# Chunked attention, then a low-rank mixer: q and k of later tiles turned by VectorE instead of TensorE

## The chip, the cores and the metric

The kernel runs on one core of a Trainium2 chip. The metric is device time in microseconds (us), from launch to end, and lower is better. Engines are named as the profile names them: PE (TensorE matmuls) and PEld (its weight loads), DVE (VectorE), ACT (ScalarE), POOL (GpSimd), SP (SyncE, which here only issues DMAs).

## The reference

```python
# q, k, v: (8, 8, 576, 64) float32: batch, heads, sequence, head dim; chunks of 64 positions
scores = scale * q_c @ k_c.T            # within each chunk only
attn = exp(scores - max) / (sum + 1e-9)
x = (attn @ v_c), heads joined          # (8, 576, 512)
xt = x.transpose(0, 2, 1)
u = x + (xt @ U @ V).transpose(0, 2, 1) # U (576, 32), V (32, 576)
out = u + relu(u @ w_ch1) @ w_ch2       # w_ch1 (512, 2048), w_ch2 (2048, 512)
```

U, V and the weights arrive as 64-bit floats and are turned into 32-bit ones on the chip. Where precision needs it, a 32-bit operand is split into a high and a low part (names ending in `h` and `l`), and a product becomes three matmuls.

## The kernel before

The batch of 8 is worked on in four pairs of sequences (`pr` = 0 to 3). A pair has 2 x 576 = 1152 positions, which are nine tiles (`t` = 0 to 8) of 128; tile 4 spans the two sequences. A tile (`pr`, `t`) goes through attention: q and k are loaded with the positions in the partitions (`load_qk`, tiles `qn`, `kn`), turned by four PE transposes of 128x128 each into `ps_qT` and `ps_kT` in PSUM (L419), copied to SBUF by ACT as `qT`, `kT` (L433), multiplied into scores (`sc`, L441), run through the softmax on DVE and ACT (`mx`, `ex`), turned again (`ps_eT`, `eT`) and multiplied by v (`av`, L472). The result is `x`. The low-rank part (`y`, `u`) and one more transpose (`ut`) follow.

Nearly all PE work is the mixer behind it. The columns of the hidden layer are cut into 16 blocks (`f`), the tiles of a pair into three groups of three (`g`). One block is `hidden` (twelve matmuls `h` of 128x384, L638), relu with the split into `hh` on ACT and `hl` on DVE, and `project_out` (nine matmuls `o` of 128x512, L664). There are 4 x 3 x 16 = 192 blocks. The attention of later tiles is woven into the blocks of earlier ones.

Two things set the order. Everything of pair 0, with the rounding of the weights from 64 to 32 bits and the first two tiles of pair 1, is placed by a small planner: an `Op` has an engine, a cost, predecessors and the buffers that it takes, and `order()` plays the list through and writes the instructions down in the order of their starts. After that, `plan()` lists the steps of each group of 16 blocks and spreads them over the blocks; there the framework's scheduler settles the order within each engine's queue, with a priority to what was written first.

Three things matter for what follows. Pair 0's nine tiles are "early": they have buffers of their own (`qkv`), and the change leaves them alone. The other 27 tiles take `qn`, `kn`, `vn`, `qT`, `kT`, `ex`, `eT` from eight shared buffers (`slot`). And all of their loads, the weight loads (`wraw`, L325 and L329) and the stores of the result go through SP's queue in order: an instruction there that waits holds up all behind it. Each DMA from SP also counts its completion on one of eight semaphores in turn, and waits until the DMA eight places before it on that queue has landed.

In the chain of a weight block, `wraw` is loaded, ACT begins the rounding (L86), five DVE instructions end it (L101), and ACT and DVE split it into `w` (L348, L351). The blocks that need weight block `f` come in the order of `STRETCHES`: for two groups in turn, so that a weight block serves two blocks of 4.2 us.

Of the kernel before, what the change touches and what calls it, by code (L numbers as in the profile page):

```python
# [10 lines left out]
F32 = mybir.dt.float32  # L11
# [10 lines left out]
def kernel(  # L22
# [11 lines left out]
    nc = tc.nc  # L34
    B, H, S, D = q.shape
# [19 lines left out]
    NPAIR = B // 2  # L55
# [13 lines left out]
    def slot(dtype, name, shape=(P, 512)):  # L69
        return work.tile(list(shape), dtype, tag="slot", name=name, bufs=NS)  # L70
# [40 lines left out]
    rank = [0]  # L111
# [260 lines left out]
    x_of = {}  # L372
    y_of = {}
    ut_of = {}

    def load_qk(pr, t):
        n = f"{pr}_{t}"
        if early(pr, t):
            words = wslot((4 * DM,), F32, "qkv_" + n)
            qn, kn = (words[:, z * DM : (z + 1) * DM].rearrange("p (h d) -> p h d", h=H) for z in range(2))  # L380
            vn = words[:, 2 * DM : 2 * DM + H * D1].rearrange("p (c a k) -> p c a k", c=2, k=D1)
        else:
            qn = slot(F32, "qn_" + n, (P, H, D))
            kn = slot(F32, "kn_" + n, (P, H, D))
            vn = slot(F32, "vn_" + n, (P, 2, HP, D1))
        nc.gpsimd.memset(vn[:, :, :, D:], 1.0)  # L386
        for r, m, b, s0 in segments(pr, t):
            nc.sync.dma_start(qn[r : r + m], q[b, :, s0 : s0 + m, :].rearrange("h s d -> s h d"))
            nc.sync.dma_start(kn[r : r + m], k[b, :, s0 : s0 + m, :].rearrange("h s d -> s h d"))
        loaded[pr, t] = qn, kn, vn  # L390

    def load_v(pr, t, behind=None):
        vn = loaded[pr, t][2]
        for c in range(2):
            b, s0 = divmod(t * P + c * C, S)
            b += 2 * pr
            for e in range(2):
                queue = nc.gpsimd if early(pr, t) else nc.sync
                d = queue.dma_start(
                    vn[e * C : (e + 1) * C, c, :, 0:D],  # L400
                    v[b, e::2, s0 : s0 + C, :].rearrange("h s d -> s h d"),
                )
                if behind is not None and c == e == 0:
                    sync = mybir.DependencyInfo(mybir.DependencyClass.Sync, mybir.DependencyReason.DATA)
                    tc.add_manual_dep(d.ins, behind.ins.name, sync, reason="q and k go first")

    def load(pr, t):
        load_qk(pr, t)
        load_v(pr, t)

    def attention_ops(pr, t, after=None):
        n = f"{pr}_{t}"
        st = {}
        mine = early(pr, t)

        def transpose(src, name):
            ps = st[name] = bank("ps_" + name + n)
            for j in range(4):
                o = nc.tensor.transpose(  # L419
                    ps[:, j * P : (j + 1) * P], src[:, j * P : (j + 1) * P], ident  # L420
                )
            if mine and name == "qT_":
                q_last[t] = o

        def evacuate(name):
            if name[0] == "e" or not mine:
                dst = slot(F32, name + n, (P, HP, P))
            elif name[0] == "q":
                st["qk"] = wslot((2, HP, P), F32, "qkT_" + n)
                dst = st["qk"][:, 0]  # L430
            else:
                dst = st["qk"][:, 1]
            nc.scalar.copy(dst.rearrange("p a b -> p (a b)"), st[name])  # L433
            st[name] = dst
# [51 lines left out]

        def scaled(e):
            if e == 0:
                st["x"] = work.tile([P, HP, 2, D], F32, tag="x", name="x_" + n, bufs=NX)
            nc.vector.tensor_mul(  # L490
                st["x"][:, :, e, :],
                st["av"][e][:, :, 0:D],
                st["sm"][:, e].unsqueeze(2).broadcast_to([P, HP, D]),
            )
            if e == 1:
                x_of[pr, t] = st["x"].rearrange("p a b k -> p (a b k)")

        src = lambda z: loaded[pr, t][z].rearrange("p h d -> p (h d)")
        flat = lambda: st["ex"].rearrange("p a b k -> p (a b k)")
        lq = Op("SP", 3.4, lambda: load_qk(pr, t), after, take="w" if mine else "slot slot slot", lat=1.6)  # L500
        tq = Op("PE", 0.55, lambda: transpose(src(0), "qT_"), lq, begun.get((pr, t - 2)), take="bank")
        lv = Op(
            "POOL" if mine else "SP",
            2.5,
# [2 lines left out]
            lat=2.2,  # L507
        )
        if mine:
            tqs[t], lvs[t] = tq, lv  # L510
        cq = Op("ACT", 0.58, lambda: evacuate("qT_"), tq, take="w" if mine else "slot", free="bank")
        tk = Op("PE", 0.55, lambda: transpose(src(1), "kT_"), lq, tq, take="bank")
        ck = Op("ACT", 0.58, lambda: evacuate("kT_"), tk, cq, take="" if mine else "slot", free="bank")
        sc = Op("PE", 0.62, scores, ck, take="bank bank", free="w" if mine else "slot slot slot slot")
        m0 = Op("DVE", 0.41, lambda: maximum(0), sc, take="slot mx")
        s0 = Op("DVE", 0.41, lambda: subtract(0), m0, free="bank")
        m1 = Op("DVE", 0.41, lambda: maximum(1), s0)
        s1 = Op("DVE", 0.41, lambda: subtract(1), m1, free="bank mx")
        ex = Op("ACT", 0.63, exp, s1)
        te = Op("PE", 0.55, lambda: transpose(flat(), "eT_"), ex, take="bank", free="slot")  # L520
        ce = Op("ACT", 0.58, lambda: evacuate("eT_"), te, take="slot", free="bank")
# [2 lines left out]
        x0 = Op("DVE", 0.415, lambda: scaled(0), sm, free="bank")  # L524
        x1 = Op("DVE", 0.415, lambda: scaled(1), x0, free="bank sm")
        begun[pr, t] = te
        return [[lq, lv], [tq, cq], [tk, ck], [sc, m0, s0, m1, s1, ex], [te, ce], [av, sm, x0, x1]]

    ybank = {}
    q_last, tqs, lvs, ahead = {}, {}, {}, {}  # L530
# [99 lines left out]
    def hidden(pr, g, f):  # L630
        uh, ul = ut_of[pr, g]
        ps = bank(f"h_{pr}_{g}_{f}")
        w = w1[f]
        prods = [(0, uh), (0, ul), (1, uh)]
        n = 0
        for cc in range(NCC):
            for z, u in prods:
                nc.tensor.matmul(  # L638
                    ps[:, :GN], lhsT=w[:, z, cc], rhs=u[:, cc, :], start=(n == 0), stop=(n == 3 * NCC - 1)
                )  # L640
                n += 1
        return ps
# [75 lines left out]
    WORK = "U T3 T4 T8 T5 T2 T1 T7 T0 T6 W0 P0 P1 V M0 M1 W1 W2 W3 W4 W5 W6 W7 W8 W9 W10 W11 W12 W13 W14 W15".split()  # L718
    STRETCHES = ((0, 0, 2), (1, 0, 2), (0, 2, 3), (1, 2, 3), (0, 3, 4), (1, 3, 4), (0, 4, 5), (1, 4, 5), (0, 5, 6), (1, 5, 6), (0, 6, 7), (1, 6, 7), (0, 7, 8), (1, 7, 8), (0, 8, 9), (1, 8, 9), (0, 9, 10), (1, 9, 10), (0, 10, 11), (1, 10, 11), (0, 11, 12), (1, 11, 12), (0, 12, 13), (1, 12, 13), (0, 13, 14), (1, 13, 14), (0, 14, 16), (1, 14, 16))
    GATES = (28, 30)  # L720
    BASE = 1000
    u_done = None
    v_done = []
# [30 lines left out]
        lvs[b].after.append(tqs[a])  # L754
    prev = None
    blocks = 0
    gates = dict(zip(GATES, range(len(GATES))))
    for g, f0, f1 in STRETCHES:
        for f in range(f0, f1):
            rank[0] = BASE  # L760
            prev = block_ops(0, g, f, f == 0, f == NF - 1, [*w_done[f], *mixed[g]], prev)
            blocks += 1
            if (g, f) == (0, NF - 1):
                last = prev
            if blocks in gates:
                rank[0] = 0
                attention_ops(1, gates[blocks], prev[0])
    assert blocks == 2 * NF
    rank[0] = 0
    for t in range(6, NT):  # L770
# [122 lines left out]
```

## Time and profile before

| | |
|---|---|
| runs | 1002.82 us median of three (1000.29 to 1005.15) |
| profiled execution | span 1000.9 us from the first to the last instruction; no time of its own is given outside the span |
| PE busy | 980.2 us (98%) |
| DVE busy | 405.6 us (41%) |
| ACT busy | 256.9 us (26%) |
| mean granted PE clock | 0.994 |
| q and k loads of the 27 later tiles | 60 DMAs, 256 KB each (128 KB where a tile spans two sequences) |

A row of a group of instructions gives the line, engine and operation, output and inputs, shape, count, then busy time and the mean of one in ns, then the idle time of the engine just before and what ended it. A row of the timeline or of the chain gives start, length, and the instruction, with a count where several stand together. A row of a window gives its bounds and length, the busy time of PE, PEld, DVE, ACT and POOL with instruction counts, the granted clock, the mean busy share of the 16 DMA engines, and GB/s.

### The profile page before, as it was taken

How to read it: one execution, taken by the hardware profiler on the slowest of the kernel's cores; microseconds unless marked ns; L12 is line 12 of the kernel's file. 1: busy time of each engine (PE TensorE's matmuls, PEld its weight loads, DVE VectorE, ACT ScalarE, POOL GpSimd, SP SyncE). 2: the span in 40 equal slices, each digit the busy share in tenths (PEclk: the TensorE clock that was granted, in tenths of full speed). 3: DMA queues.
4: the chain of work that ended last, by engine and by line, in shares of the span. 5: the costliest groups of instructions: out<-in, count | busy, mean ns of one | idle time of the engine just before them, and what ended most of it. 6: DMA issues, size and time to landing. Idle time of an engine off the chain costs nothing.

```text
span 1000.9 us, 16704 instructions
## 1 busy us (share of the span) xinstructions
PE 980.2 (98%) x7073; PEld 854.2 (85%) x7073; DVE 405.6 (41%) x813; ACT 256.9 (26%) x460; POOL 33.3 (3%) x89
## 2 busy tenths in 40 slices
PE   7799999999999999999999999999999999999998
PEld 4569999888888889888888898888888889989997
DVE  5789999652332434222333332322423233211211
ACT  4533433322322222221222221221322221111110
POOL 6500000000000000000000000000000000000000
PEclk8999999999999999999999999999999999999999
DMA  9962223152312102121120111021021000000000
GB/s 223 225 207 73 97 84 115 23 148 54 64 33 64 32 5 60 32 46 52 35 62 35 30 32 32 35 62 33 32 65 32 32 1 1 32 1 1 32 1 32
DMA packets 121914, 56.42 MB, mean 56 GB/s; under 512 B 106208, under 2 KB 114432, under 8 KB 121840
## 3 DMA queue, kind: packets, MB, share of 16 engines
q1 hardware_dynamic: 120320, 52.18, 20.5%
q0 software_dynamic: 1520, 3.17, 1.5%
q8 instruction: 56, 0.92, 0.4%
q14 instruction: 18, 0.15, 0.0%
HBM read 45.83 MB, written 9.51 MB: 55 GB/s over the span
## 4 chain that ended last, share of the span: by engine, by line
PE 71%; DVE 0%; ACT 0%; DVEq 0%; issue 0%; ACTq 0%
PE h L638 31%; PE o L664 31%; PE av L472 1%; PE sc L441 1%; PE ut L604 1%; PE ps_eT L419 1%; PE ps_qT L419 1%; PE ps_kT L419 1%; PE u L592 1%; PE y L552 1%; PE y L553 1%; DVE x L676 0%; DVE ex L459 0%; ACT ex L463 0%; DVEq L888 0%; DVE mx L455 0%
## 5 line engine op out<-in xcount | busy, mean ns | idle before, releaser
L638 PE MATMUL h<-uth,w 128*128 128x384 f32 x1536 | 425.2, 341 | 0.4 <-DVE x L490 0.3
L664 PE MATMUL o<-w,hh 128*128 128x512 f32 x1152 | 363.5, 403 | 0.0
L638 PEld LDWEIGHTS h<-uth,w 128*128 128x128 f32 x1536 | 281.3, 188 | 8.5 <-issue 0.8
L651 DVE SCALAR_TENSOR_TENSOR hl<-h,hh 128x384 fp32r<-128x384 f32 x192 | 106.7, 556 | 429.9 <-ACT hh L646 429.8
L638 PE MATMUL h<-utl,w 128*128 128x384 f32 x768 | 259.4, 338 | 0.0
L664 PEld LDWEIGHTS o<-w,hh 128*128 128x128 f32 x1152 | 207.7, 188 | 34.9
L646 ACT ACTIVATE hh<-h 128x384 fp32r<-128x384 f32 x192 | 94.3, 491 | 481.9 <-PE h L638 481.8
L664 PE MATMUL o<-w,hl 128*128 128x512 f32 x576 | 217.7, 395 | 0.0
L638 PEld LDWEIGHTS h<-utl,w 128*128 128x128 f32 x768 | 144.4, 188 | 6.3 <-DVE utl L617 0.3
L664 PEld LDWEIGHTS o<-w,hl 128*128 128x128 f32 x576 | 108.3, 188 | 24.8
L463 ACT ACTIVATE ex<-ex 128x512 f32<-128x512 f32 x36 | 22.7, 632 | 87.4 <-DVE ex L459 87.3
L455 DVE TENSOR_REDUCE mx<-sc 128x4 f32<-128x256 f32 x72 | 27.9, 417 | 31.7 <-PE sc L441 31.7
L598 DVE TENSOR_TENSOR x<-u,x 128x512 f32<-128x512 f32 x36 | 24.3, 684 | 27.1 <-PE u L592 26.8
L617 DVE TENSOR_TENSOR utl<-ut,uth 128x512 fp32r<-128x512 f32 x36 | 24.4, 688 | 20.3 <-ACT uth L612 20.3
L433 ACT COPY eT<-ps_eT 128x512 f32<-128x512 f32 x36 | 21.0, 587 | 37.4 <-PE ps_eT L419 37.2
L545 DVE TENSOR_TENSOR xl<-x,xh 128x512 fp32r<-128x512 f32 x30 | 20.5, 688 | 23.6 <-ACT xh L541 20.5
L612 ACT CAST uth<-ut 128x512 fp32r<-128x512 f32 x36 | 20.8, 588 | 31.6 <-PE ut L604 31.6
L459 DVE TENSOR_TENSOR ex<-sc,mx 128x256 f32<-128x256 f32 x72 | 27.9, 417 | 1.2 <-DVE mx L455 0.5
L490 DVE TENSOR_TENSOR x<-av,sm 128x256 f32<-128x256 f32 x72 | 27.2, 418 | 1.1
L386 POOL MEMSET vn<- 128x8 f32 x27 | 3.0, 113 | 698.9 <-PE y L553 171.1
L676 DVE TENSOR_TENSOR x<-o,x 128x512 f32<-128x512 f32 x36 | 23.3, 684 | 5.8 <-PE o L664 5.8
L348 ACT CAST w<-wroom 128x1024 fp32r<-128x1024 f32 (+1 forms) x19 | 17.1, 915 | 27.4 <-DVE wroom L101 27.4
(88 smaller groups left out, 606.6 us busy)
## 6 DMA issues: line engine op xcount, KB each, us to landing
wraw<-in_moe_w_ch_dram SPq DMA_DIRECT2D x32, 512.0 KB, 4.7
out_dram<-x SPq DMA_DIRECT2D x36, 256.0 KB, 2.1
vn<-in_v_dram SPq DMA_DIRECT2D x108, 64.0 KB, 2.8
qn<-in_q_dram SPq DMA_DIRECT2D x24, 256.0 KB, 3.4
kn<-in_k_dram SPq DMA_DIRECT2D x24, 256.0 KB, 4.0
qkv<-in_v_dram POOLq DMA_DIRECT2D x36, 64.0 KB, 6.6
qkv<-in_q_dram SPq DMA_DIRECT2D x8, 256.0 KB, 8.9
qkv<-in_k_dram SPq DMA_DIRECT2D x8, 256.0 KB, 8.0
```

Of the source, the lines that this page charges most:

```text
L419: o = nc.tensor.transpose(ps[:, j * P : (j + 1) * P], src[:, j * P : (j + 1) * P], ident)
L455: nc.vector.reduce_max(mx, st["sc"][e], axis=AX.X)
L459: nc.vector.tensor_sub(st["ex"][:, :, e, :], st["sc"][e], mx.unsqueeze(2).broadcast_to([P, HP, C]))
L463: nc.scalar.activation(exf, exf, AF.Exp, scale=SCALE)
L490: nc.vector.tensor_mul(st["x"][:, :, e, :], st["av"][e][:, :, 0:D], st["sm"][:, e].unsqueeze(2).broadcast_to([P, HP, D]),)
L598: nc.vector.tensor_add(x, st["u"], x)
L617: nc.vector.tensor_sub(ul[:, :, js], st["t"].rearrange("p (c t) -> p c t", c=NCC), uh[:, :, js])
L638: nc.tensor.matmul(ps[:, :GN], lhsT=w[:, z, cc], rhs=u[:, cc, :], start=(n == 0), stop=(n == 3 * NCC - 1))
L646: nc.scalar.activation(hh, ps[:, :GN], AF.Relu)
L651: nc.vector.scalar_tensor_tensor(hl, ps[:, :GN], 0.0, hh, op0=ALU.max, op1=ALU.subtract)
L664: nc.tensor.matmul(acc[g, j], lhsT=h[:, js], rhs=w2[f][:, z], start=(first and i == 0), stop=(final and i == 2),)
L676: nc.vector.tensor_add(x, ps, x)
```

## The change

For the 27 later tiles, q and k no longer go through PE. DVE can transpose, but only within squares of 32x32. So the data is brought into an arrangement in which that is enough: a new function `halve` copies half of the head dim (32 of 64 values) of q or k of one sequence from HBM to an HBM scratch tensor `half...` of shape (576, 8 x 32), in runs of 128 B; there are eight such transfers for a pair, 24 in all. `load_qk` then reads from the scratch 32 positions at a time into 32 partitions, in runs of 512 B, with four DMAs for each of q and k (eight for the tile that spans two sequences). Two DVE instructions (`squares`, L460) turn `qn` and `kn` into `qT` and `kT`. The heads now stand in another order (0 to 3 in the upper partitions, 4 to 7 in the lower, instead of even and odd ones), and v's loads and x's columns follow (`heads`).

Each `halve` waits for the last `hidden` matmul written before it. For pair 1 the planner places the eight transfers, one after each block from the fourth on; for pairs 2 and 3 they are written behind the load of the next tile, one or two per tile. The planner's first tiles of pair 1 wait for the last of the eight.

```diff
+    def halve(b, z, g):
+        d = halves[b, z, g] = dram.tile([S, H * SQ], F32, name=f"half{'qk'[z]}_{b}_{g}")
+        moved = nc.sync.dma_start(
+            d.rearrange("s (h i) -> s h i", h=H),
+            (q, k)[z][b, :, :, g * SQ : (g + 1) * SQ].rearrange("h s i -> s h i"),
+        )
+        sync = mybir.DependencyInfo(mybir.DependencyClass.Sync, mybir.DependencyReason.DATA)
+        tc.add_manual_dep(moved.ins, hidden_last[0].ins.name, sync, reason="after this block")
+
+    def halvings(pr):
+        return [lambda b=b, z=z, g=g: halve(b, z, g) for b in (2 * pr, 2 * pr + 1) for z in range(2) for g in range(2)]
...
+        if not early(pr, t):
+            for z, dst in enumerate((qn, kn)):
+                for r, m, b, s0 in segments(pr, t):
+                    for e in range(2):
+                        for g in range(2):
+                            x0 = (2 * e + g) * SQ
+                            nc.sync.dma_start(
+                                dst[x0 : x0 + SQ, r // SQ : (r + m) // SQ, :],
+                                halves[b, z, g][s0 : s0 + m, e * P : (e + 1) * P].rearrange(
+                                    "(a j) c -> j a c", j=SQ
+                                ),
+                            )
...
+        def squares(z, name):
+            dst = slot(F32, name + n, (P, HP, P))
+            nc.vector.transpose(
+                dst.rearrange("p h (a j) -> p h a j", j=SQ),
+                loaded[pr, t][z].rearrange("p a (h i) -> p h a i", i=SQ),
+            )
+            st[name] = dst
...
+        if mine:
+            cq = Op("ACT", 0.58, lambda: evacuate("qT_"), tq, take="w", free="bank")
...
+        else:
+            ck = Op("DVE", 0.6, lambda: squares(1, "kT_"), tq, take="slot")
+            turned = [[tq], [ck]]
...
+    HALVES_FROM = 4
...
+            if blocks >= HALVES_FROM and second:
+                rank[0] = 0
+                in_halves = Op("SP", 0.6, second.pop(0), prev[0], lat=6.0)
...
+                pr, t = tiles[i]
+                if pr + 1 < NPAIR:
+                    todo = to_halve.setdefault(pr + 1, halvings(pr + 1))
+                    for _ in range(-(-len(todo) // max(1, NT - 1 - t))):
+                        todo.pop(0)()
```

PE, in a regular stretch of pair 1's mixer, at tile 1 of pair 2. Before, between the hidden blocks 4 and 5 of group 1:

```order
L638 MATMUL h_1_4_4038<-uth_1_3622,w_1207 128x384
L419 MATMUL ps_qT_1_4055<-ident,qn_1_3695 128x128 x4
L664 MATMUL o_3_3947<-w_1141,hh_1_3_4008 128x512 x2
L664 MATMUL o_3_3947<-w_1141,hl_1_3_4010 128x512
L664 MATMUL o_4_3951<-w_1141,hh_1_3_4008 128x512 x2
L664 MATMUL o_4_3951<-w_1141,hl_1_3_4010 128x512
L664 MATMUL o_5_3955<-w_1141,hh_1_3_4008 128x512 x2
L664 MATMUL o_5_3955<-w_1141,hl_1_3_4010 128x512
L419 MATMUL ps_kT_1_4071<-ident,kn_1_3696 128x128 x4
L638 MATMUL h_1_5_4078<-uth_1_3622,w_1273 128x384
```

Now:

```order
L690 MATMUL h_1_4_4052<-uth_1_3630,w_1213 128x384
L716 MATMUL o_3_3953<-w_1143,hh_1_3_4014 128x512 x2
L716 MATMUL o_3_3953<-w_1143,hl_1_3_4016 128x512
L716 MATMUL o_4_3957<-w_1143,hh_1_3_4014 128x512 x2
L716 MATMUL o_4_3957<-w_1143,hl_1_3_4016 128x512
L716 MATMUL o_5_3961<-w_1143,hh_1_3_4014 128x512 x2
L716 MATMUL o_5_3961<-w_1143,hl_1_3_4016 128x512
L690 MATMUL h_1_5_4082<-uth_1_3630,w_1283 128x384
```

The two groups of four transposes are gone, and the `o` matmuls after the fourth hidden block still read the `hl` of the third.

SP among the weight loads (`wraw_1093` and the next ones are weight blocks 7, 8 and so on). Before:

```order
L325 DMA wraw_1093<-in_moe_w_ch_dram 128x4x256
L329 DMA wraw_1093<-in_moe_w_ch_dram 128x1024
L325 DMA wraw_1162<-in_moe_w_ch_dram 128x4x256
L329 DMA wraw_1162<-in_moe_w_ch_dram 128x1024
L325 DMA wraw_1228<-in_moe_w_ch_dram 128x4x256
L329 DMA wraw_1228<-in_moe_w_ch_dram 128x1024
```

Now:

```order
L326 DMA wraw_1093<-in_moe_w_ch_dram 128x4x256
L330 DMA wraw_1093<-in_moe_w_ch_dram 128x1024
L382 DMA halfq_0_1120<-in_q_dram 4608x1x32
L382 DMA halfq_1_1162<-in_q_dram 4608x1x32
L326 DMA wraw_1166<-in_moe_w_ch_dram 128x4x256
L330 DMA wraw_1166<-in_moe_w_ch_dram 128x1024
L382 DMA halfk_0_1190<-in_k_dram 4608x1x32
L382 DMA halfk_1_1232<-in_k_dram 4608x1x32
L326 DMA wraw_1236<-in_moe_w_ch_dram 128x4x256
L330 DMA wraw_1236<-in_moe_w_ch_dram 128x1024
```

Ahead of each of the weight blocks 8, 9, 10 and 11 stand two transfers that were not there.

SP at tile 4 of pair 1, the one that spans two sequences. Before:

```order
L679 DMA out_dram<-x_5_737 128x512
L399 DMA vn_4_2354<-in_v_dram 64x4x64
L388 DMA qn_4_2352<-in_q_dram 64x8x64
L389 DMA kn_4_2353<-in_k_dram 64x8x64
L388 DMA qn_4_2352<-in_q_dram 64x8x64
L389 DMA kn_4_2353<-in_k_dram 64x8x64
L399 DMA vn_4_2354<-in_v_dram 64x4x64 x3
```

Now, from the last loads of tile 3 to the seventh and eighth of q:

```order
L432 DMA vn_3_2298<-in_v_dram 64x4x64 x4
L382 DMA halfq_0_2312<-in_q_dram 4608x1x32
L382 DMA halfq_1_2314<-in_q_dram 4608x1x32
L409 DMA qn_4_2366<-halfq_0_1120 32x2x128
L409 DMA qn_4_2366<-halfq_1_1162 32x2x128
L409 DMA qn_4_2366<-halfq_0_1120 32x2x128
L409 DMA qn_4_2366<-halfq_1_1162 32x2x128
L409 DMA qn_4_2366<-halfq_0_1257 32x2x128
L409 DMA qn_4_2366<-halfq_1_1302 32x2x128
L409 DMA qn_4_2366<-halfq_0_1257 32x2x128
L409 DMA qn_4_2366<-halfq_1_1302 32x2x128
```

Two transfers for pair 2 stand ahead of the tile's loads; the seventh and eighth load of q are eight places behind them, and eight loads of k and four of v follow.

More of the change, by code (lines that the diff above doesn't have):

```diff
@@ L41 @@
     C = 64
+    SQ = 32
     D1 = D + 1
@@ L374 @@
     ut_of = {}
+    halves = {}
+    hidden_last = [None]
+    def halve(b, z, g):
[8 more added lines that the diff above has]
+        return [lambda b=b, z=z, g=g: halve(b, z, g) for b in (2 * pr, 2 * pr + 1) for z in range(2) for g in range(2)]
     def load_qk(pr, t):
@@ L382, in load_qk @@
         else:
-            qn = slot(F32, "qn_" + n, (P, H, D))
-            kn = slot(F32, "kn_" + n, (P, H, D))
+            qn = slot(F32, "qn_" + n, (P, P // SQ, P))
+            kn = slot(F32, "kn_" + n, (P, P // SQ, P))
             vn = slot(F32, "vn_" + n, (P, 2, HP, D1))
         nc.gpsimd.memset(vn[:, :, :, D:], 1.0)
+        if not early(pr, t):
[10 more added lines that the diff above has]
+                            )
+            loaded[pr, t] = qn, kn, vn
+            return
         for r, m, b, s0 in segments(pr, t):
@@ L390, in load_qk, with heads @@
         loaded[pr, t] = qn, kn, vn
+    def heads(pr, t, e):
+        return slice(e, None, 2) if early(pr, t) else slice(e * HP, (e + 1) * HP)
     def load_v(pr, t, behind=None):
@@ L400, in load_v @@
                     vn[e * C : (e + 1) * C, c, :, 0:D],
-                    v[b, e::2, s0 : s0 + C, :].rearrange("h s d -> s h d"),
+                    v[b, heads(pr, t, e), s0 : s0 + C, :].rearrange("h s d -> s h d"),
                 )
@@ L409, in load, with attention_ops @@
         load_v(pr, t)
-    def attention_ops(pr, t, after=None):
+    def attention_ops(pr, t, *after):
         n = f"{pr}_{t}"
@@ L423, in transpose @@
                 q_last[t] = o
+        def squares(z, name):
[5 more added lines that the diff above has]
+            st[name] = dst
         def evacuate(name):
-            if name[0] == "e" or not mine:
+            if name[0] == "e":
                 dst = slot(F32, name + n, (P, HP, P))
@@ L488, in scaled @@
             if e == 0:
-                st["x"] = work.tile([P, HP, 2, D], F32, tag="x", name="x_" + n, bufs=NX)
+                st["x"] = work.tile([P, DM], F32, tag="x", name="x_" + n, bufs=NX)
+            by_head = st["x"].rearrange("p (h d) -> p h d", h=H)
             nc.vector.tensor_mul(
-                st["x"][:, :, e, :],
+                by_head[:, heads(pr, t, e), :],
                 st["av"][e][:, :, 0:D],
@@ L495, in scaled @@
             if e == 1:
-                x_of[pr, t] = st["x"].rearrange("p a b k -> p (a b k)")
-        src = lambda z: loaded[pr, t][z].rearrange("p h d -> p (h d)")
+                x_of[pr, t] = st["x"]
+        src = lambda z: loaded[pr, t][z].rearrange("p a b -> p (a b)")
         flat = lambda: st["ex"].rearrange("p a b k -> p (a b k)")
-        lq = Op("SP", 3.4, lambda: load_qk(pr, t), after, take="w" if mine else "slot slot slot", lat=1.6)
-        tq = Op("PE", 0.55, lambda: transpose(src(0), "qT_"), lq, begun.get((pr, t - 2)), take="bank")
+        lq = Op(
+            "SP", 3.4 if mine else 5.0, lambda: load_qk(pr, t), *after, take="w" if mine else "slot slot slot", lat=1.6
+        )
+        if mine:
+            tq = Op("PE", 0.55, lambda: transpose(src(0), "qT_"), lq, begun.get((pr, t - 2)), take="bank")
+        else:
+            tq = Op("DVE", 0.6, lambda: squares(0, "qT_"), lq, begun.get((pr, t - 2)), take="slot")
         lv = Op(
@@ L510, in attention_ops @@
             tqs[t], lvs[t] = tq, lv
-        cq = Op("ACT", 0.58, lambda: evacuate("qT_"), tq, take="w" if mine else "slot", free="bank")
-        tk = Op("PE", 0.55, lambda: transpose(src(1), "kT_"), lq, tq, take="bank")
-        ck = Op("ACT", 0.58, lambda: evacuate("kT_"), tk, cq, take="" if mine else "slot", free="bank")
+        if mine:
+            cq = Op("ACT", 0.58, lambda: evacuate("qT_"), tq, take="w", free="bank")
+            tk = Op("PE", 0.55, lambda: transpose(src(1), "kT_"), lq, tq, take="bank")
+            ck = Op("ACT", 0.58, lambda: evacuate("kT_"), tk, cq, free="bank")
+            turned = [[tq, cq], [tk, ck]]
+        else:
+            ck = Op("DVE", 0.6, lambda: squares(1, "kT_"), tq, take="slot")
+            turned = [[tq], [ck]]
         sc = Op("PE", 0.62, scores, ck, take="bank bank", free="w" if mine else "slot slot slot slot")
@@ L526, in attention_ops @@
         begun[pr, t] = te
-        return [[lq, lv], [tq, cq], [tk, ck], [sc, m0, s0, m1, s1, ex], [te, ce], [av, sm, x0, x1]]
+        return [[lq, lv], *turned, [sc, m0, s0, m1, s1, ex], [te, ce], [av, sm, x0, x1]]
     ybank = {}
@@ L637, in hidden @@
             for z, u in prods:
-                nc.tensor.matmul(
+                hidden_last[0] = nc.tensor.matmul(
                     ps[:, :GN], lhsT=w[:, z, cc], rhs=u[:, cc, :], start=(n == 0), stop=(n == 3 * NCC - 1)
@@ L756 @@
     blocks = 0
+    second = halvings(1)
     gates = dict(zip(GATES, range(len(GATES))))
@@ L764 @@
                 last = prev
+            if blocks >= HALVES_FROM and second:
+                rank[0] = 0
+                in_halves = Op("SP", 0.6, second.pop(0), prev[0], lat=6.0)
             if blocks in gates:
+                assert not second
                 rank[0] = 0
-                attention_ops(1, gates[blocks], prev[0])
+                attention_ops(1, gates[blocks], prev[0], in_halves)
     assert blocks == 2 * NF
@@ L790 @@
     manual.__exit__(None, None, None)
+    to_halve = {}
     tiles = [(pr, t) for pr in range(NPAIR) for t in range(NT)]
```

## The prediction

> **What bounds the kernel now.** I read the busy times and slices first, then windows by stage, then the chain of waits, then single rows around the lines that change.
>
> ```profile
> span 1000.9 us, 16704 instructions
> PE 980.2 (98%) x7073; PEld 854.2 (85%) x7073; DVE 405.6 (41%) x813; ACT 256.9 (26%) x460; POOL 33.3 (3%) x89
> PE   7799999999999999999999999999999999999998
> PEclk8999999999999999999999999999999999999999
> DMA  9962223152312102121120111021021000000000
> 75.00:100.00 25.00, 25.00 (x128) 22.57 (x127) 24.08 (x30) 9.70 (x13) 0.00 (x0) 1.00 0.22 71
> 225.00:250.00 25.00, 24.73 (x245) 20.94 (x245) 7.25 (x22) 6.33 (x12) 0.11 (x1) 1.00 0.26 55
> 300.00:400.00 100.00, 100.00 (x693) 88.60 (x692) 34.20 (x72) 23.84 (x45) 0.34 (x3) 1.00 0.15 40
> ```
>
> TensorE is busy 98% at a granted clock that is full nearly throughout. The last three rows are windows (length, then PE, PEld, DVE, ACT, POOL busy, clock, DMA share, GB/s). From 75 us on PE has no gap to speak of: a microsecond of PE work removed is a microsecond of span, unless a new wait takes its place. Two stages differ. At 75:100 DVE is full too (24.08 of 25), since it still rounds the weights; from 225 on it is a third busy. So I price the change on PE first, then look in each stage for the wait that could end last instead.
>
> **What the removed PE work costs.** "Busy" of a matmul overlaps its neighbour, so the price comes from the chain (start, length), where a piece counts only what it adds:
>
> ```profile
> 401.19 2.11 PE h L638 x12
> 403.30 0.44 PE ps_qT L419 x4
> 403.73 2.09 PE o L664 x9
> 405.83 0.44 PE ps_kT L419 x4
> 406.26 2.12 PE h L638 x12
> ...
> 964.93 2.11 PE h L638 x12
> 967.05 2.09 PE o L664 x9
> 969.14 2.11 PE h L638 x12
> ```
>
> A clean block lasts 969.14 - 964.93 = 4.21 us; the one with both transposes of a tile 406.26 - 401.19 = 5.07. The difference, 0.86, is two groups of four transposes at 0.43 each. How many go:
>
> ```profile
> L419 PE MATMUL ps_qT<-ident,qn 128*128 128x128 f32 x108 | 17.1, 274 | 0.0
> L419 PE MATMUL ps_kT<-ident,kn 128*128 128x128 f32 x108 | 16.2, 273 | 0.7 <-ACT qT L433 0.7
> L433 ACT COPY kT<-ps_kT 128x512 f32<-128x512 f32 x27 | 15.9, 588 | 17.3 <-PE ps_kT L419 16.5 <-DMA kn<-in_k_dram 0.8
> L545 DVE TENSOR_TENSOR xl<-x,xh 128x512 fp32r<-128x512 f32 x30 | 20.5, 688 | 23.6 <-ACT xh L541 20.5 <-PE y L552 1.4 <-issue 1.3
> L92 DVE TENSOR_SCALAR wroom<-wroom 128x512 f32<-128x512 f32 x6 | 2.5, 418 | 0.0
> ```
>
> 216 transposes are 54 groups: 54 x 0.43 = **23.2 us off PE**, all at places where PE is full. The 54 copies on ACT (588 ns) go too; ACT is a quarter busy and ends no stage, so that is worth nothing.
>
> **What VectorE takes over.** 54 transposes of 128x512 f32 in SBUF. No row has one. One source in SBUF took 418 ns, two sources 688; those are my ends. By its one source it is nearer to 418; I take 688, since the result hangs on neither and the dearer one tests the cover. That is 37 us, all after 190 us, where DVE is idle two thirds of the time. The cover: in the regular order the `o` matmuls that read `hl` of a block stand behind the `h` of the next block (2.11 us of PE), so one transpose, even two, ahead of `hl` on DVE delays nobody. In the denser places a few tenths may be lost; they are in the range. Regrouping v's heads and x's columns leaves instruction counts and sizes as they were: nothing.
>
> **The loads.** A tile's q and k are 8 DMAs (16 for the tile that spans two sequences) instead of 2 or 4, on the same SP queue, each waiting in turn. The shortest distances from issue to use before:
>
> ```profile
> 217.00 1.45 SPq L679 DMA_DIRECT2D out_dram<-x  x2
> 225.19 1.95 SPq L399 DMA_DIRECT2D vn<-in_v_dram  x3
> 246.44 0.69 PE L441 MATMUL sc<-kT,qT 64*64 64x64 f32 x32
> 259.96 0.54 SPq L388 DMA_DIRECT2D qn<-in_q_dram  x1
> 269.66 0.66 PE L419 MATMUL ps_qT<-ident,qn 128*128 128x128 f32 x4
> 486.79 0.48 SPq L388 DMA_DIRECT2D qn<-in_q_dram  x1
> 503.01 0.60 PE L419 MATMUL ps_qT<-ident,qn 128*128 128x128 f32 x4
> ...
> qn<-in_q_dram SPq DMA_DIRECT2D x24, 256.0 KB, 3.4
> ```
>
> SP issues one DMA in 0.65 us (three in 1.95). q then lands 4 x 0.65 + 3.4 = 6.0 us after the first issue, k 8.6. In pairs 2 and 3 the closest tile has 16.2 us (486.79 to 503.01): hidden. Tile 6 of pair 1 has 9.7 for q: hidden.
>
> **The new HBM-to-HBM transfers.** 24 of them, each 4608 runs of 128 B in and out. No row shows such a run. Nearest:
>
> ```profile
> DMA packets 3168, 0.79 MB, mean 143 GB/s; under 512 B 3168, under 2 KB 3168, under 8 KB 3168
> q1 hardware_dynamic: 3168, 0.79, 70.4%
> ...
> q1 hardware_dynamic: 672, 1.05, 39.3%
> ```
>
> The first two rows are the window 343.5:349, loads in 256 B packets: 0.704 x 16 engines x 5.5 us / 3168 = 19.6 ns a packet. The last is 96:104, one weight load in 1 to 4 KB packets: 0.393 x 8 = 3.1 us of all engines, 6.0 ns per 128 B. So a transfer takes T = 288 packets per engine x 6.0 ns = 1.7 us at the least; at the most each run costs a small packet twice, once read and once written, 39 ns, T = 11.3. I take 17 ns, T = 5: the runs are nearest to the 256 B packets, with half the bytes. A load's fixed part is 3.4 - 1024/16 x 0.0196 = 2.1 us.
>
> *Early.* Eight of them go between the weight loads, two ahead of each, released by the 4th to 11th block. SP takes DMAs in order, and the engines too, so the weights queue behind them. Tightest is weight block 11:
>
> ```profile
> 83.87 0.49 ACT L646 ACTIVATE hh<-h 128x384 fp32r<-128x384 f32 x1 [1.62 <-PE h L638]
> 119.77 0.37 SPq L325 DMA_DIRECT2D wraw<-in_moe_w_ch_dram  x1
> 141.02 1.14 ACT L86 ACTIVATE wroom<-wraw 128x1024 f32<-128x1024 f32 x1
> 153.08 1.23 DVE L351 TENSOR_TENSOR w<-wroom,w 128x1024 fp32r<-128x1024 f32 x1
> 165.85 0.49 ACT L646 ACTIVATE hh<-h 128x384 fp32r<-128x384 f32 x1 [4.35 <-PE h L638]
> ```
>
> The first row is the 4th block's end, the start of the first transfer. With all eight and weights 8 to 11 in one line, block 11 lands at 83.9 + 8T + 4 x 3.1 + 2.1 = 98.4 + 8T: at T = 5, 138.4, before it is wanted at 141.0. Behind that PE has a margin of its own: the weights were ready at 154.3, and the block that uses them began at 165.85 - 2.11 = 163.7, so 9.4 us. Nothing is lost up to T = 6.5; the whole 23.2 us up to T = 9.4. At T = 5: **0**. Its ends are 0 and 98.4 + 90.4 - 150.4 = 38.4.
>
> *Tile 4 of pair 1.* On SP two transfers now stand ahead of its 16 loads, and SP's DMAs carry one of eight completion counters in turn, so the 7th and 8th load wait until the two transfers have landed. Behind the last `out` of that stage (217.7, 2.6 earlier after six removed groups) come ten loads, 6.5 us, so the transfers go at 222; they land at 222 + 2T + 2 = 234; eight loads of k take 5.2, landing 3.4, a transpose with its handover 0.9: kT at 243.5, 4 to 5 us later than now relative to PE. PE wants it at 246.44 - 10 x 0.43 = 242.1. **1.4 us lost** (0 at T = 1.7, 14 at T = 11.3); I add 1 for DVE, which sits at q's transpose meanwhile with the softmax sums of the tile before behind it. The other 14 transfers stand ahead of loads with 16 us or more to spare. The wait for a block delays only what is behind it on SP, and the block is one PE has already reached.
>
> **The sum.** -23.2 + 0 + 2.4 = -20.8. The profiled span is 1000.9, so 980.1; the three runs' median is 1002.82, 1.9 above the span, so **982 us**.
>
> **Rivals.** (a) *All hidden*: T of 3 us or less and nothing waits: 1002.8 - 23.2 = 979.6. For it: DMA share of 0.15. (b) *Weights late*: T between 6.5 and 9.4; at T = 8 block 11 lands at 162.4, PE loses 12.0, and the total is 991.6. For it: DVE has no slack at 75:175 in which to catch up. (c) *Slower*: the same queue at T = 11.3 costs 38.4: 1018. It decides from T = 9.4, 33 ns a run. For it: small packets already cost four times as much per byte as large ones do. Against it: those 19.6 ns include the ramp of a load. The Trainium skill (DMA: Bandwidth & Descriptors, Specifications) puts line rate at 512 B and up and says that below it the engine reads, modifies and writes. By that rule a run of 128 B would be paid about twice, by estimate the 1018 us of (c). The 256 B rows agree that small is dear, but they write to SBUF; no run here shows a small write to HBM. (d) *No gain*: DVE's queue holds up `hl` in each tile and PE waits there what it waited for the transposes, 54 x 0.43, about 1003; against it stands the third of DVE's time in use.
>
> **Chances.** Forecast 0.58, (a) 0.20, (b) 0.12, (c) 0.07, (d) 0.03. Half a percent (5 us) is what a measurement here can tell from no change. The forecast, (a) and most of (b) are faster: 0.88; the end of (b) with (d) is same: 0.05; (c) is slower: 0.07. The range leaves out (c), (d) and the upper half of (b): from 976 ((a), less the 3 us by which runs scatter) to 994.
>
> **What would show it.** After the change: no ps_qT and ps_kT with qn, kn; blocks of 4.21 us plus eT, ut, sc, av only; DVE transposes near 0.4 to 0.7 us; a landing of T + 2, about 7 us, on the half transfers; PE full at 75:175; a gap of 1 to 3 us before the scores near 240 us. Wrong, if PE idles before `h` at 130 to 190 us with a weight load's landing above 15 us, or if `sc` waits for a kT in most tiles.

## The result, and the profile after

The changed kernel takes 987.58 us (median of four runs, 984.5 to 988.33), the kernel before 1001.56 on the same chip: a ratio of 0.985, 95% interval 0.982 to 0.987. That is 14.0 us faster, within the forecast range and 5.6 above the 982 forecast.

Rows of the page of the changed kernel: span, busy times, one of the two groups of VectorE's new transposes, and two DMA issues with KB each and median us to landing.

```profile
span 982.7 us, 16528 instructions
PE 961.3 (98%) x6854; PEld 835.0 (85%) x6857; DVE 439.5 (45%) x867; ACT 227.5 (23%) x406; POOL 33.7 (3%) x89
L460 DVE STREAM_TRANSPOSE qT<-qn 128x512 f32<-128x512 f32 x27 | 19.1, 708 | 31.8 <-PE y L604 15.6
wraw<-in_moe_w_ch_dram SPq DMA_DIRECT2D x32, 512.0 KB, 7.1
qn<-halfq SPq DMA_DIRECT2D x96, 64.0 KB, 2.0
```

PE is still busy 98%, with 18.9 us less work. But the weight loads now take 7.1 us to land, 4.7 before: something in the early stage has moved.

To see where time comes and goes, count the 192 blocks by their `hh` on ACT, one per block, numbered from 0, and compare their starts. Timeline rows of blocks 0, 28 and 191, of the kernel before and then of the changed one:

```profile
70.02 0.49 ACT L646 ACTIVATE hh<-h 128x384 fp32r<-128x384 f32 x1 [1.52 <-PE h L638]
191.08 0.49 ACT L646 ACTIVATE hh<-h 128x384 fp32r<-128x384 f32 x1 [2.09 <-PE h L638]
992.14 0.49 ACT L646 ACTIVATE hh<-h 128x384 fp32r<-128x384 f32 x1 [3.71 <-PE h L638]
```

```profile
67.24 0.50 ACT L698 ACTIVATE hh<-h 128x384 fp32r<-128x384 f32 x1 [1.52 <-PE h L690]
195.13 0.49 ACT L698 ACTIVATE hh<-h 128x384 fp32r<-128x384 f32 x1 [2.09 <-PE h L690]
973.74 0.49 ACT L698 ACTIVATE hh<-h 128x384 fp32r<-128x384 f32 x1 [3.71 <-PE h L690]
```

Block 0 starts 2.8 us earlier, but nothing that the change touches runs before it, and the experiments below scatter there by up to 2.9 us either way: I take it for the start of an execution and leave it out. From block 0 to 28 the changed kernel **loses 6.8 us** (127.89 against 121.06), all of it between 104 and 128 us; from 28 to 191 it **gains 22.45** (778.61 against 801.06).

The gain can be split. Windows from block 28 to 191, in two halves (bounds, length, then PE busy), before and after:

```profile
191.10:623.60 432.50, 430.16 (x3331) 377.08 (x3330) 144.66 (x333) 108.52 (x203) 2.15 (x19) 1.00 0.20 48
623.60:992.10 368.50, 368.50 (x2349) 328.54 (x2348) 96.91 (x202) 70.80 (x135) 0.67 (x6) 1.00 0.09 24
```

```profile
195.15:611.07 415.92, 415.26 (x3180) 362.14 (x3179) 169.38 (x372) 87.84 (x164) 2.25 (x20) 1.00 0.35 73
611.07:973.70 362.63, 362.58 (x2285) 322.25 (x2284) 105.65 (x216) 61.82 (x119) 0.56 (x5) 1.00 0.08 25
```

PE's busy time falls from 798.66 to 777.84: 20.8 us, on average 0.386 for each of the 54 groups. Its idle time falls from 2.34 to 0.71: another 1.6.

The loss has its rows too. Rows of SP's queue in the changed kernel (start, length, instruction), from the first transfers on:

```profile
81.00 8.99 SPq L382 DMA_DIRECT2D halfq<-in_q_dram  x2
90.09 3.27 SPq L326 DMA_DIRECT2D wraw<-in_moe_w_ch_dram  x1
93.95 5.99 SPq L382 DMA_DIRECT2D halfk<-in_k_dram  x2
99.99 3.42 SPq L326 DMA_DIRECT2D wraw<-in_moe_w_ch_dram  x1
110.33 3.67 SPq L326 DMA_DIRECT2D wraw<-in_moe_w_ch_dram  x1
```

ACT at the same place, where L87 begins the rounding of a weight block, and the one wait of PE:

```profile
108.90 1.13 ACT L87 ACTIVATE wroom<-wraw 128x1024 f32<-128x1024 f32 x1 [4.19 <-DMA wraw<-in_moe_w_ch_dram]
119.11 1.12 ACT L87 ACTIVATE wroom<-wraw 128x1024 f32<-128x1024 f32 x1 [5.50 <-DMA wraw<-in_moe_w_ch_dram]
120.13 0.48 ACT L698 ACTIVATE hh<-h 128x384 fp32r<-128x384 f32 x1
```

```profile
120.66 1.22 PE L716 MATMUL o<-w,hh 128*128 128x512 f32 x2 [3.52 <-ACT hh L698]
```

The chain reads: the load goes out late, ACT stands at L87 for 4.19 and then 5.50 us, `hh` of a block that needs no new weights is queued behind it on ACT, and PE waits for that `hh`. One wait of 3.52 us does not make 6.8. Windows of 4 us give the rest (the column ahead of the last two is the granted clock):

```profile
116.00:120.00 4.00, 1.14 (x5) 0.57 (x3) 2.12 (x3) 0.89 (x1) 0.00 (x0) 0.97 1.18 309
120.00:124.00 4.00, 3.34 (x8) 2.67 (x9) 3.32 (x5) 1.67 (x3) 0.00 (x0) 0.50 1.32 166
124.00:128.00 4.00, 4.00 (x17) 3.81 (x16) 1.93 (x2) 0.09 (x1) 0.00 (x0) 0.68 1.03 247
```

After the gap PE runs at half clock: 3.34 x 0.50 + 4.00 x 0.32 = 3.0 us, and with 1.14 x 0.03 and the 3.52 that is 6.5 of the 6.8. The Trainium skill (TensorE: Matmul & The Clock Gate, Part 1: The HAM clock gate) says that the clock falls to a half after an idle window of about 3.4 us and returns after a busy one. The trace agrees in kind, with 0.50 behind a gap of 3.52 us; but in x2 below the clock is at 0.50 behind a gap of 2.98 us as well, so these runs do not bear out 3.4 us as the least gap that costs clock.

### The profile page after: what moved, and what is told of

Same layout as the page of the kernel before. It is cut to its first block, busy times and chain, and to the rows that moved or that the text cites. A ratio compares the mean times of both kernels' runs of the same rounds, so it can differ in the third digit from the quotient of the medians.

```text
span 982.7 us, 16528 instructions
## 1 busy us (share of the span) xinstructions
PE 961.3 (98%) x6854; PEld 835.0 (85%) x6857; DVE 439.5 (45%) x867; ACT 227.5 (23%) x406; POOL 33.7 (3%) x89
## 4 chain that ended last, share of the span: by engine, by line
PE 91%; DMA 3%; DVE 3%; ACT 1%; SPq 1%; issue 1%; POOL 0%; DVEq 0%; ACTq 0%; POOLq 0%
PE h L690 41%; PE o L716 40%; PE sc L482 2%; PE av L513 2%; PE ut L656 2%; PE ps_eT L452 1%; DMA wraw<-in_moe_w_ch_dram 1%; PE u L644 1%; DMA qkv<-in_k_dram 1%; PE y L604 1%; PE y L605 1%; DMA uraw<-in_moe_U_dram 1%; DMA qkv<-in_v_dram 1%; PE y L611 1%; ACT qkT L474 0%
## 5 line engine op out<-in xcount | busy, mean ns | idle before, releaser
L716 PE MATMUL o<-w,hh 128*128 128x512 f32 x1152 | 359.2, 401 | 3.7 <-ACT hh L698 3.5
L716 PEld LDWEIGHTS o<-w,hh 128*128 128x128 f32 x1152 | 211.6, 189 | 42.2 <-ACT hh L698 5.6
L650 DVE TENSOR_TENSOR x<-u,x 128x512 f32<-128x512 f32 x36 | 24.3, 684 | 27.6 <-PE u L644 27.4
L460 DVE STREAM_TRANSPOSE qT<-qn 128x512 f32<-128x512 f32 x27 | 19.1, 708 | 31.8 <-PE y L604 15.6
```

Of the source, the lines that this page charges most:

```text
L650: nc.vector.tensor_add(x, st["u"], x)
L716: nc.tensor.matmul(acc[g, j], lhsT=h[:, js], rhs=w2[f][:, z], start=(first and i == 0), stop=(final and i == 2),)
```

## The experiments

Time lost (+) or gained (-) against the kernel before, in us, from the starts of the blocks as above, in one profiled execution of each kernel; the medians are of several runs in five rounds, except in the two kernels marked *, which ran once. The kernel before, on the same chips, had medians of 1002.79 (beside x1 to x4) and 1002.58 (x5 to x8), and 1003.32 in one run (x9). The early loss of kernels that are alike up to block 28 (changed, x5, x6) is 6.55 to 7.15, so differences of 0.3 there mean nothing; the third column repeats to 0.02 where nothing that matters to it was changed (x1, x2, x7, x9).

| kernel | time | ratio, 95% interval | blocks 0 to 28 | 28 to 191 |
|---|---|---|---|---|
| changed kernel | 987.58 | 0.982 to 0.987 | +6.83 | -22.45 |
| x1: no hold for pair 1 | 982.36 | 0.978 to 0.981 | 0.00 | -22.45 |
| x2: pair 1's transfers on POOL | 988.35 | 0.985 to 0.988 | +8.60 | -22.47 |
| x3: no scratch | 1018.56 | 1.015 to 1.017 | -0.01 | +15.07 |
| x4: transfers alone | 1011.59 | 1.007 to 1.010 | +6.12 | +0.75 |
| x5: 18 more groups on PE | 994.90 | 0.990 to 0.993 | +6.55 | -15.53 |
| x6: 36 more turns on VectorE | 988.52 | 0.983 to 0.988 | +7.15 | -22.01 |
| x7: long runs * | 980.85 | | 0.00 | -22.45 |
| x8: holds alone | 1002.93 | 0.999 to 1.001 | -0.01 | -0.01 |
| x9: POOL, long runs * | 980.66 | | 0.00 | -22.44 |

**x1, the hold taken away.**

```diff
-        tc.add_manual_dep(moved.ins, hidden_last[0].ins.name, sync, reason="after this block")
+        if b > 3:
+            tc.add_manual_dep(moved.ins, hidden_last[0].ins.name, sync, reason="after this block")
```

> The changed kernel, with pair 1's eight transfers at the same places of SP's queue, but not held for a block of the mixer; the sixteen of pairs 2 and 3 keep their hold. Between 104 and 128 us the changed kernel loses 6.8 us against the kernel before, and there three `wraw` loads of the mixer's weights end the waits of ACT. Theory H (the hold): SP stands at a transfer until its block has ended, and weight loads queued behind it are issued that much later; without the hold SP issues the transfer and then the load, the late weights are in time, and the loss of 6.8 us goes: about 981 us, ACT's waits before the rounding (line L87) between 75 and 150 us under 3 us in sum. Rival B (the transfers themselves): 4 us of service and the bytes crowd the weight loads wherever they are issued, so the loss stays within 1.5 us of 6.8: 986 to 989 us, and ACT's waits before L87 stay near 11 us.

The loss is gone to the hundredth and nothing else moved. SP's queue, and the group of L87 between 75 and 150 us with its idle time (11.3 us in the changed kernel):

```profile
54.09 9.76 SPq L382 DMA_DIRECT2D halfq<-in_q_dram  x2
63.95 3.27 SPq L326 DMA_DIRECT2D wraw<-in_moe_w_ch_dram  x1
74.20 3.27 SPq L326 DMA_DIRECT2D wraw<-in_moe_w_ch_dram  x1
```

```profile
L87 ACT ACTIVATE wroom<-wraw 128x1024 f32<-128x1024 f32 x9 | 10.3, 1143 | 0.0
```

The first transfers go at 54.09, not at 81, and the weight load behind them 26 us earlier. At 982.36 us it is the fastest of the kernels that compute q and k of the reference. Theory H is borne out, so far: rival B's crowding "wherever they are issued" is not there.

**x4, the transfers alone, in the kernel before.** `halve`, its holds and their places are added; nothing reads the scratch.

> The kernel before, with the 24 transfers added and each held as in the change, and nothing that reads the scratch: q and k are still turned by TensorE. It prices the transfers alone. If the early loss is due to them (theory H or rival B), 6.8 us are lost by block 28 and nothing later: about 1008 us. If it is due to the order in which the changed kernel's other instructions stand, no loss: 1000 to 1003 us. If the diffuse loss of 2.5 us after block 28 is due to traffic of pairs 2 and 3, the sum is nearer to 1010.

6.1 us are lost by block 28, so the loss is the transfers', not that of the new order of PE or VectorE. (The medians differ by 8.8 us, the blocks by 6.9; the profiled execution reached block 0 2.5 us later than that of the kernel before, which the blocks leave out.) The 0.8 later falls at blocks 36 to 38 near 250 us. From block 48 on nothing is lost: the transfers of pair 3 are hidden.

**x8, the holds alone.** As x4, but a transfer is 2 KB:

```diff
-            d.rearrange("s (h i) -> s h i", h=H),
-            (q, k)[z][b, :, :, g * SQ : (g + 1) * SQ].rearrange("h s i -> s h i"),
+            d[0:16, 0:SQ],
+            (q, k)[z][b, 0, 0:16, g * SQ : (g + 1) * SQ],
```

> The kernel before, with the 24 holds at the same places of SP's queue, but each held transfer is 16 runs of 128 bytes (2 KB) in place of 4608 (576 KB), and nothing reads it. Theory H: SP stands at the holds as before and the weight loads go out late; 5 to 7 us are lost by block 28, about 1008 us, nearly as with the whole transfers (8.8 us by the medians, 6.1 by the blocks). Rival B: without bytes there is no crowding, no loss, 1002 to 1004 us. In between: the transfers' own 4 us stand in front of the weight loads as well, and the loss is 3 to 5 us.

Theory H fails here. SP stands just as long, and no time is lost:

```profile
86.66 8.92 SPq L382 DMA_DIRECT2D halfq<-in_q_dram  x2
95.67 0.54 SPq L326 DMA_DIRECT2D wraw<-in_moe_w_ch_dram  x1
```

```profile
L87 ACT ACTIVATE wroom<-wraw 128x1024 f32<-128x1024 f32 x9 | 10.3, 1147 | 1.3 <-DMA wraw<-in_moe_w_ch_dram 1.3
```

The weight load goes out as late as in the changed kernel (this execution started 5.6 us later), but its issue takes 0.54 us in place of 3.27.

**x7, the same bytes in long runs.**

```diff
-            d.rearrange("s (h i) -> s h i", h=H),
-            (q, k)[z][b, :, :, g * SQ : (g + 1) * SQ].rearrange("h s i -> s h i"),
+            d.rearrange("(h r) c -> h (r c)", h=HP),
+            (q, k)[z][b, g * HP : (g + 1) * HP].rearrange("h s d -> h (s d)"),
```

> The changed kernel, whose 24 transfers move the same 576 KB in long runs (four whole heads, one after the other) in place of 4608 runs of 128 bytes; the scratch then holds other numbers, and q and k of the later tiles are not those of the reference. It prices the short runs: a transfer takes 4 us now. If the runs of 128 bytes cost it, a transfer takes 3 us or less here; if bytes alone count, about 4. Theory H (the hold costs, not the transfer): the loss between 104 and 128 us stays within 1 us of 6.8 whatever the transfer takes. Rival B: it falls in step with the transfer's time.

Again no loss, with the holds in place. The queue of one transfer alone, in the changed kernel (window 81:91) and here (85:87), with packets, MB and share of 16 engines, and the first weight loads behind transfers here:

```profile
q1 hardware_dynamic: 4800, 0.61, 43.0%
```

```profile
q1 hardware_dynamic: 16, 0.59, 81.0%
93.20 0.54 SPq L326 DMA_DIRECT2D wraw<-in_moe_w_ch_dram  x1
101.56 0.58 SPq L326 DMA_DIRECT2D wraw<-in_moe_w_ch_dram  x1
```

0.430 x 10 us = 4.3 us of all engines for 4800 packets, 14.3 ns a packet, so 4.1 us for a transfer; in long runs 0.81 x 2 = 1.6 us. Both this run and x8 contradict H as I had put it, and x1 contradicts B. What holds is that **it takes both**: with the hold but long runs nothing is lost (x7), with the short runs but no hold neither (x1).

The queue's rows show how the two meet. PE uses up a weight block every two blocks, 8.4 us. With the holds and little behind them, SP keeps that pace: 93.20 to 101.56 is 8.4 us here. With the short runs the issue of each weight load takes 3.3 to 3.7 us in place of 0.5, and SP takes 9.9 and 10.3 us from one weight load to the next in the changed kernel (90.09, 99.99, 110.33), slower than PE needs them. Without the hold the pace is no better, 10.3 us (63.95, 74.20), but SP begins 26 us earlier (32 counted from block 0) and has that lead to lose. The hold takes away the lead, the short runs take away the pace.

The loads themselves are not what is slow: between 88 and 122 us the second DMA of a weight block (L330; L329 before) lands a median of 5.1 us after its issue in the changed kernel, 4.7 before, and 6.2 here, where nothing is lost. So the delay stands on SP ahead of that DMA. Why SP needs 3.3 us or more for an issue behind short runs, and whether it waits there for the engines to serve them (4.1 us a transfer), no run shows.

**x2, POOL's queue.** `nc.sync` becomes `nc.gpsimd` for pair 1's transfers, and their `Op` stands on POOL.

> The changed kernel, with pair 1's eight transfers issued from POOL's queue in place of SP's, each held for the same block of the mixer as before. Theory H: SP's queue no longer stands at a hold, weight loads go out as they did before the change, and a transfer of 4 us lands beside them; the loss of 6.8 us goes, about 981 us. Rival B (the transfers' own service and bytes crowd the weight loads): the loss stays, 986 to 989 us. A third, P: POOL stands in the hold with work of the mixer queued behind it (its instructions are few, 89 in all, 33.7 us), and PE then waits for POOL: a loss of some other size, seen as waits that POOL ends.

No gain over the changed kernel, for another reason: no wait is left before L87 (0.0), but 8.6 us are lost. POOL and VectorE at 100 us, and VectorE's group between 75 and 130 us (688 ns in x1):

```profile
99.25 2.19 POOL L382 DMA_DIRECT2D halfk<-in_k_dram  x1 [2.79 <-PE h L690]
100.93 2.74 POOL L382 DMA_DIRECT2D halfq<-in_q_dram  x1
```

```profile
100.47 3.72 DVE L100 TENSOR_SCALAR wraw<-wroom 128x1024 uint32<-128x1024 uint32 x1
```

```profile
L100 DVE TENSOR_SCALAR wraw<-wroom 128x1024 uint32<-128x1024 uint32 x6 | 8.2, 1375 | 0.1
```

The two issues keep POOL until 103.67, and the instruction of VectorE that began in the first ends 0.5 us after the second. In this stage VectorE is full, so `hl` is late. PE's longest wait for it, and the window behind:

```profile
104.70 0.80 PE L716 MATMUL o<-w,hl 128*128 128x512 f32 x1 [2.98 <-DVE hl L703]
104.00:108.00 4.00, 3.30 (x8) 2.62 (x9) 3.93 (x6) 0.93 (x1) 0.00 (x0) 0.50 1.03 215
```

By block 8, 6.4 us are lost: this wait of 2.98, one of 0.28 before it, and the half clock behind, 3.30 x 0.50 + 4.00 x 0.31 = 2.9 (0.69 from 108 to 112 us).

**x9, POOL's queue and long runs.**

> Pair 1's eight transfers issued from POOL's queue, with their holds, and all 24 moving the same 576 KB in long runs in place of 4608 runs of 128 bytes (the scratch then holds other numbers, and q and k of the later tiles are not those of the reference). With the short runs on POOL the trace has each issue at 2.2 to 2.7 us of POOL, and instructions of VectorE on one operand (L93, L94, L100), which take 0.69 us elsewhere, at up to 3.72 us beside them; PE then waits for `hl`, and 8.5 us are lost by block 12. Theory D: POOL writes the runs' list one by one, and VectorE's one-operand instructions stand still while it does; with few runs an issue takes under 1 us, VectorE's instructions stay at 0.69 us, and no time is lost by block 28 (within 1 us). Rival Q: the loss comes from the holds on POOL's queue or from the bytes; it stays above 4 us.

```profile
92.89 0.49 POOL L382 DMA_DIRECT2D halfk<-in_k_dram  x1
```

```profile
L100 DVE TENSOR_SCALAR wraw<-wroom 128x1024 uint32<-128x1024 uint32 x7 | 4.8, 692 | 0.1
```

Theory D is borne out: with 16 runs in place of 4608 the issue takes 0.49 us, L100 is back at 692 ns, and nothing is lost, with the holds and the bytes as they were.

**x3, no scratch.** The 24 transfers are gone, and each load reads its runs of 128 B from q and k:

```diff
-                            nc.sync.dma_start(
-                                dst[x0 : x0 + SQ, r // SQ : (r + m) // SQ, :],
-                                halves[b, z, g][s0 : s0 + m, e * P : (e + 1) * P].rearrange(
-                                    "(a j) c -> j a c", j=SQ
-                                ),
-                            )
+                            for a in range(m // SQ):
+                                nc.sync.dma_start(
+                                    dst[x0 : x0 + SQ, r // SQ + a, :].rearrange("j (h i) -> j h i", i=SQ),
+                                    (q, k)[z][
+                                        b, e * HP : (e + 1) * HP, s0 + a * SQ : s0 + (a + 1) * SQ, g * SQ : (g + 1) * SQ
+                                    ].rearrange("h j i -> j h i"),
+                                )
```

> The changed kernel without the scratch and without the 24 transfers: each later tile's loads read q and k as they lie, in runs of 128 bytes, with 32 loads in place of 8 (one for each block of 32 rows). PE, ACT and VectorE do what they do in the changed kernel. Theory H and rival B both have nothing left to lose early, so 979 to 982 us, if SP's queue (32 issues of 0.46 us, 14.7 us for a tile of some 24 us) and the runs of 128 bytes are hidden behind a tile. Rival S: SP's queue is too long and loads of v and stores behind it come late: PE waits for k's turn by VectorE, and the time is 985 us or more. The diffuse loss of 2.5 us from block 28 to the end should stay if it is due to the order of PE's instructions, and shrink if it is due to the transfers.

Rival S. Between blocks 28 and 48 (pair 1's tiles 2 to 6 lie there) 27.6 us are lost where the changed kernel gains 9.1. Rows of SP and PE:

```profile
230.74 7.75 SPq L410 DMA_DIRECT2D qn<-in_q_dram  x16
238.60 8.57 SPq L410 DMA_DIRECT2D kn<-in_k_dram  x16
```

```profile
228.44 1.13 PE L483 MATMUL sc<-kT,qT 64*64 64x64 f32 x32 [7.92 <-DVE kT L461]
```

The 32 issues take SP 16.3 us, and with v's loads it is 19.2 to the next tile's first load, at 249.96; the kernel before went through the same five tiles in 85.7 us (blocks 32 to 48), 17.1 each. So SP is the slower one: VectorE's turns of k wait 31.3 us for their loads between 190 and 335 us, PE waits for the turns, and between blocks 28 and 48 it has a mean clock of 0.90. From block 48 on the direct loads gain 12.5 against 13.4: there they are nearly hidden. So the scratch earns its keep where tiles are dense, by needing a quarter of the issues.

**x5, more work on PE.** One group of four transposes of `ident` into a bank that nobody reads, at q's place, in pairs 2 and 3.

> The changed kernel, with one group of four transposes of the identity on TensorE more for each of the 18 tiles of pairs 2 and 3, at the place of q's turn, with nothing that reads it. From block 28 to the end the change took 22.5 us, of which PE's busy time gave 20.8 (0.386 us for each of the 54 groups) and less idle time 1.6; the forecast had 0.43 for a group. Theory M (a group is worth less than its place in the chain, since what is left is split more often): each extra group costs 0.39, 6.9 us in all, 994.5 us. Theory F (a group is worth 0.43, and something else in the changed kernel gives 2.4 back): 7.7 us, 995.3 us. The two are told apart by the time of the blocks in the trace, which agrees within 0.1 us between runs, not by the medians. Rival N (TensorE has slack): no cost.

22.45 - 15.53 = 6.92 us for 18 groups, 0.384 on average: theory M's number. Block by block it has two parts. Against the changed kernel, 18 blocks of x5 are 0.41 to 0.45 us longer, 7.74 in all, 0.43 for each group, and two (69 and 117) are 0.44 and 0.45 shorter. In those two the scores of a tile are written in one run in x5; in the changed kernel they stand in two parts with `o` matmuls between. At block 69, changed kernel and then x5:

```profile
401.18 0.33 PE L482 MATMUL sc<-kT,qT 64*64 64x64 f32 x2
402.33 0.69 PE L482 MATMUL sc<-kT,qT 64*64 64x64 f32 x30
403.40 0.69 PE L482 MATMUL sc<-kT,qT 64*64 64x64 f32 x32
```

So a group by itself is worth 0.43, and M's reason, that what is left is split more often without the groups, holds at these two places. 54 x 0.43 is 23.2 where PE's busy time fell by 20.8: PE's other work then takes 2.4 more in the changed kernel, 0.9 of it in the scores of these two blocks. The rest was not followed.

**x6, more work on VectorE.** `squares` turns twice in pairs 2 and 3.

> The changed kernel, with VectorE turning q and k of pairs 2 and 3 twice (36 more turns of 0.70 us, 25 us more of VectorE). If VectorE has the slack that its share of 45% shows, the time stays within 1 us of the changed kernel's 987.6 us. Rival: the turns delay `hl`, on which PE's second half of a block waits, and each turn gives back part of its group; then 36 more turns cost 0.05 us or more each, 2 us or more, and PE waits for `hl` between 380 and 860 us.

36 more turns cost 0.4 us in the blocks from 28 on, and one block (97) alone is 0.46 longer, while the differences of the others cancel: VectorE's work is covered.

## Why the prediction was right, and where it was not

The time came within the range and the reason for the gain was right, but one term was missing. Against the block times -20.8 was forecast and -15.6 measured; the 5.2 between them are 6.8 for the early weights, 0.8 for PE, and 2.4 the other way for tile 4.

- **PE, -23.2: the price right, the sum a little too good.** 54 groups went, and 0.43 is what a group is worth (x5, block by block). Left out was that PE's other work is ordered anew without them: 2.4 of the 23.2 went back there, and 1.6 came from waits of PE that I had not counted, so 22.45 is left.
- **Early weights, 0: the step that failed**, measured at +6.8. "Tightest is weight block 11" is wrong. The load at 119.77 is block 11, but the transfers stand ahead of the loads issued at 59.90, 67.91, 83.05 and 96.51 before: blocks 6 to 9, counted from 0 at the first load, where the text ahead of the prediction says 8 to 11 (its `wraw_1093` is block 5, not 7). Their roundings began in the kernel before at

```profile
101.09 1.15 ACT L86 ACTIVATE wroom<-wraw 128x1024 f32<-128x1024 f32 x1
107.39 1.14 ACT L86 ACTIVATE wroom<-wraw 128x1024 f32<-128x1024 f32 x1
113.70 1.14 ACT L86 ACTIVATE wroom<-wraw 128x1024 f32<-128x1024 f32 x1
124.20 1.14 ACT L86 ACTIVATE wroom<-wraw 128x1024 f32<-128x1024 f32 x1
```

  My own line, 83.9 + 8T + 4 x 3.1 + 2.1, put on block 9, gives 131.2 at the measured T of 4.1, 7.0 after the 124.20 at which it is wanted. That it meets the 6.8 is partly luck: the line has no term for SP's issues of 3.3 us and more behind the transfers, and about 3 of the 6.8 are half clock.
- **The margin of 9.4 us on PE: did not exist.** I followed the weights to the block that needs them, and forgot what is queued behind the waiting instruction: `hh` of other blocks stands behind L87 on ACT. "The wait for a block delays only what is behind it on SP" was true, and what is behind it was the weights.
- **T = 5: 4.1**, 14.3 ns a run, between my ends of 6.0 and 39 and under my 17. The Trainium skill (DMA: Bandwidth & Descriptors, Specifications) puts line rate at 512 B and up; the trace agrees in kind, 4.1 us in runs of 128 B against 1.6 for the same bytes in long ones. The 39 ns a run of rival (c) they do not cost.
- **Tile 4 of pair 1, +2.4: about 0.** The transfers went at 223.62 as forecast (222), but the eight loads of k took SP 3.66 us, not 5.2, and landed in 2.0, not 3.4. SP, VectorE and PE of the changed kernel there:

```profile
223.62 3.96 SPq L382 DMA_DIRECT2D halfq<-in_q_dram  x2
235.78 3.66 SPq L409 DMA_DIRECT2D kn<-halfk  x8
```

```profile
241.69 0.71 DVE L460 STREAM_TRANSPOSE kT<-kn 128x512 f32<-128x512 f32 x1 [0.31 <-DMA vn<-in_v_dram]
243.42 0.69 PE L482 MATMUL sc<-kT,qT 64*64 64x64 f32 x32
```

  PE has no wait ahead of that `sc`.
- **VectorE, 0: right.** 0.71 us a turn, a little over my dearer end, and covered (x6).
- **The rivals.** The mechanism was that of (b), late weights, at a T where (b) had nothing to lose. (c) and (d) did not happen; x1 comes near the time of (a), 982.4 against 979.6, with the transfers as they were. Two of their figures were off on the prediction's own terms: 982 has tile 4's loss in it and the times of (b) and (c) have not (14 us at T = 11.3), and small packets cost 1.6 times as much per byte as large ones (19.6 ns for 256 B against 2 x 6.0), not four.

## What to carry to other kernels

In this kernel a hold and a slow transfer on a queue that issues in order were each harmless, and together cost what neither showed alone. So price them together: compare the pace of the queue with the pace at which its loads are used, and ask how much lead the hold leaves. Name the load that stands right behind by counting the queue's rows, not by its place in the text. When a load comes late, look at everything queued behind the instruction that waits for it, on that engine too. A gap of some 3 us on PE was paid for twice here, in idle time and in the clock that followed. And an average over many places (0.384) can hide a constant price (0.43) with something else that moved.

## What the runs showed of the hardware

- An issue on SP right behind a transfer of 4608 short runs takes 3.3 to 3.7 us in the changed kernel, 0.5 to 0.6 behind a long-run one of the same bytes (x7).
- POOL needs 2.2 to 2.7 us to issue such a transfer, and VectorE's one-operand instructions (0.69 us) stand still meanwhile, up to 3.72 us, while those on two operands keep their 1.22. The Trainium skill (SBUF — State Buffer, SBUF: two separate sides) describes a port pair that VectorE, in some of its instructions, and GpSimd lock for a whole instruction, while the other waits. These rows are in line with it, with VectorE as the one that waits; that the port is the cause, no run here shows.
- A gap of 3.52 us on PE cost 3.0 us more at half clock, and one of 2.98 us (x2) 2.9 more.
- A group of four 128x128 f32 transposes on PE costs 0.43 us among other matmuls (x5). One instruction of VectorE that turns 128x512 f32 in squares takes 0.71.
